# Fewer uncut score products, a first chunk of 64 rows and later low weights in a kernel of attention, feed-forward and mixture

## The chip, the core and the metric

The kernel runs on one core of a Trainium2 chip. The metric is the device time of one execution in microseconds (us). The engines are called TensorE (PE in the profile; its weight loads are PEld), VectorE (DVE), ScalarE (ACT), GpSimd (POOL) and SyncE (SP, which issues the transfers here).

## The reference

Three layers follow each other; each takes what the one before gives. Batch 4, sequence 448, model width 768.

```python
# 1. attention: 12 heads of 64, causal
scores = scale * np.matmul(q, k.transpose(0, 1, 3, 2))
scores = np.where(mask, -1000000000.0, scores)
scores = scores - np.max(scores, axis=-1, keepdims=True)
attn = np.exp(scores)
attn = attn / (np.sum(attn, axis=-1, keepdims=True) + 1e-09)
x = np.matmul(attn, v)
...
# 2. feed-forward with a gate from a convolution of 3 steps, width 1024
h = np.maximum(x @ w_in, 0.0)
for k in range(K):
    conv_out += conv_w[k][None, None, :] * hp[:, k:k + S, :]
gate = 1.0 / (1.0 + np.exp(-conv_out))
x = h * gate @ w_out
...
# 3. mixture: the best 2 of 4 experts for each position, each a causal attention head of 64
topk = np.argpartition(-(x @ w_gate), K, axis=-1)[..., :K]
for e in range(E):
    q, k, v = x @ wq[e], x @ wk[e], x @ wv[e]
    ...
    ye = a @ v @ wo[e]
    out += mask[..., None] * w[:, :, kk:kk + 1] * ye
```

All inputs are float32. The choice of experts hangs on small differences, so the products must hold nearly all of float32.

## The kernel before, in words

**Products in two halves.** A float32 matrix is cut into a high half, rounded to the fp32r type, and a low half, which is what is left (`high`, line 588, a copy; `low`, line 599, a subtraction). A product of two matrices is then three matmuls: high by high, low by high, high by low. A float32 matmul without the cut is also used, at four passes, where cutting is dearer.

**Pairs of heads.** Attention works on 24 pairs of heads, six a batch. For the pairs in `WHOLE_QK` (before: pairs 0 to 2 of the first batch) query and key are loaded as they are by `prepare_whole` (the keys in a sparse layout, by small transfers) and each score chunk is one float32 matmul a head (line 659). For the others `prepare` loads both, a high half of both is made (`ON["qk high"]`: VectorE, ScalarE or GpSimd) and two low halves (VectorE or GpSimd), and `scores` writes three matmuls a chunk and head (line 669), the two heads side by side, each with 64 rows of contraction.

**Chunks.** A pair's 448 query positions are cut in four chunks that begin at `Q0` = 0, 64, 192 and 320. Their widths `QN` are 64, 128, 128, 128, but before the change the first chunk is computed with 128 rows too, those of positions 0 to 127, and the keys up to 64. Each chunk takes a masked maximum on VectorE (line 644), an exponential on ScalarE (line 648) and a scaling by the row's sum (line 694 or 691). Then the weights are transposed on TensorE (`tr`, line 702) and multiplied by the values (`weigh`, line 761; `weigh_both`, line 747, with uncut float32 for the pairs in `WHOLE_AV`, the first eight). The transposes of the chunks are put side by side in one PSUM tile, so that those of a 128-row first chunk overlap the second's place and come before it.

**Feed-forward.** For each batch `ffn_in` makes eight groups of 18 products with 448 columns (line 896, into `pf`), each followed by: a relu on ScalarE (line 910, tile `hp`), three convolution steps (line 916 on ScalarE, 921 twice on VectorE, tile `half`), a tanh (line 936), a gate (line 929), and the gate's high and low halves (tile `pair`, lines 592 to 600). `ffn_out` makes six groups of 24 products from the eight gates and the output weights (tile `thou`), and stores its results to memory, from where the mixture loads them.

**Mixture.** `weights` (line 1021) loads the mixture's weights, makes their high halves (ScalarE or GpSimd) and their low halves (GpSimd alone), three loads for one tile `wbig` and then four for another. These start when the last attention pair's weights are scaled (`free`). Then follow, batch by batch, the queries and keys, values, four experts and the output.

**Order.** A class `Plan` collects every step with a cost for each engine that may do it. It runs a list scheduling with a rank for each step, several times, adds noise to the ranks of steps that begin in given stretches (`SHIFTS`: seed, from, to, amplitude), and writes the instructions in the order of the resulting plan. So the engine of a step, the buffers and the order of each engine's instructions come from that plan. A step begins on the chip when the data that it reads are there; a step behind it on its engine waits with it.

```python
        whole = p in WHOLE_QK
        ops = prepare_whole(p) if p in WHOLE_QK else prepare(p, ph, not whole)
        ...
        late = P.ops[-1]          # in the loop over batches: the last step of ffn_in
        ffn_out(b, gs)
        ...
        free = [NORM[B * H - 1]]  # behind the loop
```

Of the kernel before, what the change touches and what calls it, by code (L numbers as in the profile page):

```python
# [13 lines left out]
OP = mybir.AluOpType  # L14
# [24 lines left out]
WHOLE_QK = range(3)  # L39
# [11 lines left out]
SIDES = 3.6  # L51

# [15 lines left out]
def product(n):  # L68
    return 0.0034 + n * 0.000442
# [443 lines left out]
def attention_moe_moe(ctx: ExitStack, tc: tile.TileContext, qk, vv, w_in, cw, w_out, wqk, wvg, wo, out):  # L513
# [94 lines left out]
    def scores(qk, j, e, turns=False):  # L608
# [16 lines left out]
        def bank(o, c):  # L625
            return sbs[o][c][:, COL[c]:COL[c] + Q0[c] + QN[c]]

        def ec(o, c):
            n = Q0[c] + QN[c]
            if turns:  # L630
                return e[:, COL2[c]:COL2[c] + 2 * n].rearrange("p (j o d) -> p j o d", o=2, d=64)[:, :, o]
            return e[:, COL2[c] + o * n:COL2[c] + o * n + n]
# [5 lines left out]
        def weight(o, c):  # L638

            w, st, sb = Q0[c] + QN[c], sts[o], sbs[o]  # L640

            def mx(_):
                m = mask[:, 448 - w:448] if c and (o or turns) else mask[:, 320:320 + w]
                nc.vector.tensor_tensor_reduce(out=ec(o, c), in0=blocked(bank(o, c)), in1=blocked(m), scale=-0.125, scalar=3.0e38,  # L644
                                               op0=OP.add, op1=OP.min, accum_out=st[:, 0, c:c + 1])

            def ex(_):
                nc.scalar.activation(ec(o, c), ec(o, c), AF.Exp, bias=st[:, 0, c:c + 1], scale=-1.0,  # L648
                                     accum_out=st[:, 1, c:c + 1])

            P.op({"V": on_vector(w)}, mx, r=[(sb[c], c)], w=[(e, (o, c)), (st, ("m", c))])
            P.op({"A": on_scalar(w) + 0.23}, ex, r=[(st, ("m", c))], w=[(e, (o, c)), (st, ("s", c))])


        if whole:
            for o, (qs, kh, r) in enumerate(qk):
                for c in ORDER:
                    w = Q0[c] + QN[c]
                    P.op({"T": 4 * w / 2400}, lambda _, o=o, c=c, w=w, qs=qs, kh=kh: nc.tensor.matmul(
                        bank(o, c), qs()[:, Q0[c]:Q0[c] + 128], kh()[:, :w // 64], start=True, stop=True), r=r, w=[(sbs[o][c], c)])  # L660
                    weight(o, c)
        else:
            q, k, r = qk
            for two in (ORDER[:2], ORDER[2:]):
                def mm(_, two=two):
                    for c in two:
                        for i, (s, t) in enumerate(((0, 0), (1, 0), (0, 1))):
                            for o, own in enumerate(HALF):
                                nc.tensor.matmul(bank(o, c), q(s)[own, Q0[c]:Q0[c] + 128], k(t)[own, kc(o, c)], start=i == 0, stop=i == 2)  # L669

                P.op({"T": sum(SIDES * max(product(Q0[c] + QN[c]), 0.107) for c in two)}, mm, r=r,
                     w=[(sbs[o][c], c) for c in two for o in range(2)])
                for c in two:
                    for o in range(2):
                        weight(o, c)
# [4 lines left out]
    def norms(j, st, o, ec, e):  # L680
# [7 lines left out]
        for c in ORDER:  # L688
            def norm(en, c=c):
                if en == "A":  # L690
                    nc.scalar.activation(ec(o, c), ec(o, c), AF.Copy, scale=st[:, 3, c:c + 1])  # L691
                else:
                    gate = coef[:, b, c, x:x + 1] if moe else 1.0
                    engine(en).tensor_scalar(ec(o, c), ec(o, c), st[:, 3, c:c + 1], gate, op0=OP.mult, op1=OP.mult)  # L694
# [6 lines left out]
    def tr(dst, src, r, keys, m=128):  # L701
        P.op({"T": TURN}, lambda _: nc.tensor.transpose(dst(), src(), ident), r=r, w=keys, m=m)  # L702

    def transpose(e, p):
# [4 lines left out]

        for c in range(4):  # L710
            tr(lambda c=c: t0[:, Q0[c]:Q0[c] + 128], lambda n=COL2[c] + Q0[c] + QN[c]: e[:, n - 64:n + 64],
               [(e, (o, c)) for o in range(2)], [(t0, 0), (t0, 1)] if c == 0 else [(t0, c)])
# [17 lines left out]
    def weigh_both(e, v, v_r, dst):  # L730
# [3 lines left out]
        for i, use in enumerate(BLOCKS):  # L734
            t, a = P.buf("tb" if i in (1, 2) else "ta"), P.buf("ab")
            n = 0
            for j, col, q in use:
                for c in range((j + 1) // 2, 4):
                    m = COL2[c] + j * 128
                    tr(lambda t=t, x=col + Q0[c] - q: t[:, x:x + 128], lambda m=m: e[:, m:m + 128], [(e, (o, c)) for o in range(2)],  # L740
                       [(t, (j, c))] + ([(t, (j, 1))] if c == 0 else []))
# [280 lines left out]
    def weights(src, n, w, n0, keys):  # L1022
# [3 lines left out]
        P.op(copy_cost(n, "AG"), high(hi, lambda: raw[:, :n]), r=[(raw, 0)], w=[(w, (k, 0)) for k in keys])  # L1026
        P.op(two_cost(n, "G"), low(lo, lambda: raw[:, :n], hi), r=[(raw, 0)] + [(w, (k, 0)) for k in keys], w=[(w, (k, 1)) for k in keys])
# [211 lines left out]
```

## Time and profile before

| | |
|---|---|
| time, median of 3 runs (lowest to highest) | 605.22 us (605.09 to 607.0) |
| the profiled execution's own time | 602.88 us |
| its span, first to last instruction | 601.1 us |
| granted clock of TensorE | 1.00 |
| busy: PE, PEld, DVE, ACT, POOL | 577.9, 505.1, 479.0, 404.4, 190.8 us |
| share of the span | 96, 84, 80, 67, 32% |
| costliest group | 984 products of `ffn_in` and the mixture's projections, 219.8 us |
| moved by DMA | 87.78 MB, 146 GB/s |

Busy time is the union of an engine's instructions. Matmuls overlap in the records: each lasts longer than the distance to the next, so a group's sum of durations is more than its place on the engine. An idle time is put down to the step that ended last before it (the releaser). The tile names in the rows are those of buffers: `pair` holds a high and a low half, `half` raw data or convolution results, `full` raw loads, `e` the attention weights, `a` their transposes.

### The profile page before, as it was taken

Reading aid. Unit: us, or ns where it says so; the run is one execution under the profiler, and the core shown is the slowest. Engines: PE = TensorE matmul, PEld = TensorE weight load, DVE = VectorE, ACT = ScalarE, POOL = GpSimd, SP = SyncE. Lnnn points to the kernel's source line nnn. Section 1 sums busy time; section 2 is a strip of 40 time slices with the busy share of each in tenths; the row PEclk is TensorE's granted clock in tenths of the full one; section 3 lists DMA queues with packets and bytes.
Section 4 is the critical chain, followed back from the end, with each engine's and each line's share of the span. In section 5 each row is a group of like instructions: output and inputs, shape, how many; then the busy total and the mean of one; then the engine's idle time right before and its main releaser. Section 6 shows DMA issues by size and latency. Waiting matters only on the chain.

```text
span 601.1 us, 10782 instructions
## 1 busy us (share of the span) xinstructions
PE 577.9 (96%) x3577; PEld 505.1 (84%) x3580; DVE 479.0 (80%) x1353; ACT 404.4 (67%) x1035; POOL 190.8 (32%) x207
## 2 busy tenths in 40 slices
PE   8899989899999999999999999979999999999987
PEld 4577778788888988898999998868999989999877
DVE  6999999999998879987979985981156569649993
ACT  4688469888889658968868984451133268456973
POOL 4443532555663014543201631750001023002510
PEclk9999999999999999999999999999999999999999
DMA  8455534478880065672038629509733400200113
GB/s 246 146 137 150 151 103 148 131 268 286 275 270 17 1 194 190 213 256 42 2 112 270 216 89 390 136 26 352 252 92 119 152 33 2 93 1 2 63 71 145
DMA packets 50457, 87.78 MB, mean 146 GB/s; under 512 B 21856, under 2 KB 31456, under 8 KB 50400
## 3 DMA queue, kind: packets, MB, share of 16 engines
q1 hardware_dynamic: 50400, 87.09, 44.6%
q8 instruction: 28, 0.46, 0.3%
q14 instruction: 29, 0.24, 0.1%
HBM read 64.26 MB, written 22.81 MB: 145 GB/s over the span
## 4 chain that ended last, share of the span: by engine, by line
PE 56%; DVE 7%; ACT 2%; DMA 1%; issue 1%; SPq 0%; POOL 0%; ACTq 0%
PE pf L896 40%; PE po L761 5%; PE t L702 5%; PE sx L669 4%; DVE pair L600 1%; DVE half L921 1%; DMA thou<-w_scratch 1%; DVE a L600 1%; DVE e L644 1%; PE sy L669 1%; DVE half L773 1%; ACT pair L592 1%; ACT hp L910 0%; PE t L896 0%; DVE half L929 0%
## 5 line engine op out<-in xcount | busy, mean ns | idle before, releaser
L896 PE MATMUL pf<-pair,wbig 128*128 128x448 f32 x984 | 219.8, 371 | 6.2 <-ACT hp L910 3.8
L896 PEld LDWEIGHTS pf<-pair,wbig 128*128 128x128 f32 x984 | 180.2, 188 | 24.4 <-ACT hp L910 5.9
L648 ACT ACTIVATE e<-e,stat 128x448 f32<-128x448 f32 (+3 forms) x256 | 127.2, 499 | 29.0 <-DVE stat L644 28.2
L896 PE MATMUL pf<-pair,thou 128*128 128x448 f32 x576 | 131.1, 374 | 5.8 <-DVE pair L600 4.4
L896 PEld LDWEIGHTS pf<-pair,thou 128*128 128x128 f32 x576 | 105.1, 188 | 15.7 <-DVE pair L600 5.4
L600 DVE TENSOR_TENSOR a<-t,a 64x448 fp32r<-64x448 f32 (+1 forms) x96 | 75.5, 787 | 10.9 <-ACT a L592 8.8
L702 PE MATMUL t<-ident,e 128*128 128x128 f32 x512 | 81.9, 275 | 1.7 <-DVE e L694 0.7
L592 ACT ACTIVATE a<-t 64x448 fp32r<-64x448 f32 (+1 forms) x96 | 64.4, 674 | 16.5 <-PE t L702 11.2
L600 DVE TENSOR_TENSOR pair<-pf,pair 128x448 fp32r<-128x448 f32 (+3 forms) x56 | 30.1, 552 | 52.3 <-ACT pair L592 51.8
L702 PEld LDWEIGHTS t<-ident,e 128*128 128x128 f32 x512 | 61.4, 141 | 9.6 <-DVE half L594 1.2
L592 ACT ACTIVATE pair<-pf 128x448 fp32r<-128x448 f32 (+3 forms) x56 | 26.3, 486 | 59.2 <-PE pf L896 57.7
L761 PE MATMUL po<-a,thou 128*128 128x384 f32 (+5 forms) x336 | 64.3, 309 | 1.1 <-DVE half L773 1.1
L694 POOL TENSOR_SCALAR e<-e,stat,coef 128x192 f32<-128x192 f32 (+3 forms) x37 | 21.9, 605 | 131.3 <-DVE stat L687 57.7
L644 DVE CUSTOM_DVE_ANT_0 e<-sx,mask 128x64 f32<-128x64 f32 (+3 forms) x128 | 51.4, 416 | 6.1 <-PE sy L669 5.4
L921 DVE SCALAR_TENSOR_TENSOR half<-hp,cws,half 128x448 f32<-128x448 f32 x64 | 49.0, 779 | 8.2 <-ACT half L916 7.9
L644 DVE CUSTOM_DVE_ANT_0 e<-sy,mask 128x320 f32<-128x320 f32 (+3 forms) x128 | 50.7, 416 | 5.0 <-PE sy L669 3.4
L761 PEld LDWEIGHTS po<-a,thou 128*128 128x128 f32 (+1 forms) x336 | 47.6, 173 | 5.4 <-DVE half L773 2.6
L669 PE MATMUL sx<-pair,pair 64*128 64x448 f32 (+3 forms) x264 | 50.4, 306 | 0.1
L669 PE MATMUL sy<-pair,pair 64*128 64x448 f32 (+3 forms) x264 | 50.3, 306 | 0.0
L691 ACT ACTIVATE e<-e,stat 128x320 f32<-128x320 f32 (+3 forms) x104 | 46.8, 507 | 5.0 <-DVE stat L687 3.5
L648 ACT ACTIVATION_READ_ACCUMULATOR e<-e,stat 128x1 f32 x256 | 48.3, 189 | 0.0
L669 PEld LDWEIGHTS sx<-pair,pair 64*128 64x128 f32 x264 | 41.5, 185 | 4.6 <-issue 2.2
(109 smaller groups left out, 895.1 us busy)
## 6 DMA issues: line engine op xcount, KB each, us to landing
thou<-w_scratch SPq DMA_DIRECT2D x36, 512.0 KB, 5.4
x_scratch<-pair SPq DMA_DIRECT2D x24, 448.0 KB, 5.2
pair<-x_scratch SPq DMA_DIRECT2D x24, 448.0 KB, 6.0
full<-in_w_in SPq DMA_DIRECT2D x12, 512.0 KB, 4.2
full<-in_w_out SPq DMA_DIRECT2D x12, 512.0 KB, 4.8
w_scratch<-thou SPq DMA_DIRECT2D x12, 512.0 KB, 4.7
out<-half SPq DMA_DIRECT2D x24, 224.0 KB, 1.9
half<-in_vv SPq DMA_DIRECT2D x16, 256.0 KB, 4.6
```

The source lines that it names most:

```text
L592: nc.scalar.activation(dst(), src(), AF.Copy)
L600: return lambda e: engine(e).tensor_sub(dst(), src(), f32(h()))
L644: nc.vector.tensor_tensor_reduce(out=ec(o, c), in0=blocked(bank(o, c)), in1=blocked(m), scale=-0.125, scalar=3.0e38, op0=OP.add, op1=OP.mi ...
L648: nc.scalar.activation(ec(o, c), ec(o, c), AF.Exp, bias=st[:, 0, c:c + 1], scale=-1.0, accum_out=st[:, 1, c:c + 1])
L669: nc.tensor.matmul(bank(o, c), q(s)[own, Q0[c]:Q0[c] + 128], k(t)[own, kc(o, c)], start=i == 0, stop=i == 2)
L691: nc.scalar.activation(ec(o, c), ec(o, c), AF.Copy, scale=st[:, 3, c:c + 1])
L694: engine(en).tensor_scalar(ec(o, c), ec(o, c), st[:, 3, c:c + 1], gate, op0=OP.mult, op1=OP.mult)
L702: P.op({"T": TURN}, lambda _: nc.tensor.transpose(dst(), src(), ident), r=r, w=keys, m=m)
L761: lambda _: nc.tensor.matmul(ps[:n, q:S], v(k, m), rhs(), start=start, stop=stop),
L773: P.op({"V": on_vector(S)}, lambda _: nc.vector.tensor_add(xf[HALF[o], :S], ps[:64, :S], xc[HALF[0], :S]), r=[(ps, 0), (xc, 0)], w=[(xf, o)])
L896: nc.tensor.matmul(out_ap(), a(), b(), start=first, stop=end), r=r, w=[(ps, 0)])
L921: return lambda _: nc.vector.scalar_tensor_tensor(cv[:, :S], hp[:, i:S + i], cws[:, fc, i:i + 1], cv[:, :S], op0=OP.mult, op1=OP.add)
```

## The change

1. `WHOLE_QK` holds pair 0 alone; pairs 1 and 2 go through `prepare` and have cut score products.
2. The first chunk has 64 rows in all its steps: scores, masked maximum, exponential, scaling and transposes. Its transpose takes 64 rows of contraction and writes 64 columns, and no longer overlaps the second chunk's.
3. The mixture's high weights are made by ScalarE alone, and each low half waits for `late`, the low half of the last gate of the last `ffn_in`.
4. The planner's cost of a score group is another, `SHIFTS` has 37 other entries, and so the whole order is new.

```diff
-WHOLE_QK = range(3)
+WHOLE_QK = range(1)
...
-SIDES = 3.6
...
-    (50226, 530, 540, 1), (2079, 416, 436, 2), (83136, 282, 292, 1), (43264, 499, 539, 1), (58582, 209, 229, 1),
+    (42011, 517, 527, 2), (39824, 301, 321, 2), (93157, 66, 86, 5), (8490, 203, 243, 0.5), (81995, 460, 470, 2),
...
         def bank(o, c):
-            return sbs[o][c][:, COL[c]:COL[c] + Q0[c] + QN[c]]
+            return sbs[o][c][:QN[c], COL[c]:COL[c] + Q0[c] + QN[c]]
...
-            return e[:, COL2[c] + o * n:COL2[c] + o * n + n]
+            return e[:QN[c], COL2[c] + o * n:COL2[c] + o * n + n]
...
-                        bank(o, c), qs()[:, Q0[c]:Q0[c] + 128], kh()[:, :w // 64], start=True, stop=True), r=r, w=[(sbs[o][c], c)])
+                        bank(o, c), qs()[:, Q0[c]:Q0[c] + QN[c]], kh()[:, :w // 64], start=True, stop=True), r=r, w=[(sbs[o][c], c)])
...
-                                nc.tensor.matmul(bank(o, c), q(s)[own, Q0[c]:Q0[c] + 128], k(t)[own, kc(o, c)], start=i == 0, stop=i == 2)
-
-                P.op({"T": sum(SIDES * max(product(Q0[c] + QN[c]), 0.107) for c in two)}, mm, r=r,
+                                nc.tensor.matmul(bank(o, c), q(s)[own, Q0[c]:Q0[c] + QN[c]], k(t)[own, kc(o, c)], start=i == 0, stop=i == 2)
+
+                P.op({"T": 0.09 + sum(3 * max(product(Q0[c] + QN[c]), QN[c] / 1200) for c in two)}, mm, r=r,
...
-    def tr(dst, src, r, keys, m=128):
-        P.op({"T": TURN}, lambda _: nc.tensor.transpose(dst(), src(), ident), r=r, w=keys, m=m)
+    def tr(dst, src, r, keys, n=128):
+
+        P.op({"T": TURN}, lambda _: nc.tensor.transpose(dst()[:, :n], src()[:n], ident[:n, :n]), r=r, w=keys)
...
-               [(e, (o, c)) for o in range(2)], [(t0, 0), (t0, 1)] if c == 0 else [(t0, c)])
+               [(e, (o, c)) for o in range(2)], [(t0, c)], QN[c])
...
-                       [(t, (j, c))] + ([(t, (j, 1))] if c == 0 else []))
+                       [(t, (j, c))], QN[c])
...
-        P.op(copy_cost(n, "AG"), high(hi, lambda: raw[:, :n]), r=[(raw, 0)], w=[(w, (k, 0)) for k in keys])
-        P.op(two_cost(n, "G"), low(lo, lambda: raw[:, :n], hi), r=[(raw, 0)] + [(w, (k, 0)) for k in keys], w=[(w, (k, 1)) for k in keys])
+        P.op(copy_cost(n, "A"), high(hi, lambda: raw[:, :n]), r=[(raw, 0)], w=[(w, (k, 0)) for k in keys])
+
+        P.op(two_cost(n, "G"), low(lo, lambda: raw[:, :n], hi), r=[(raw, 0)] + [(w, (k, 0)) for k in keys], w=[(w, (k, 1)) for k in keys],
+             after=[late])
```

The lines that are left out slice the masks, the sums and the scaling to `QN[c]` rows in the same way. In the changed kernel line numbers from 649 on are one lower (895 for 896), and from `weights` on one higher.

How the order of the instructions moves is shown at three places. The first is GpSimd around the last convolution: `pair` with `half` are low halves of gates, `wbig` with `full` the mixture's weights (L596 is a high half, L600 a low one). Before:

```order
L596 TENSOR_SCALAR pair_107<-half_135 128x448
L600 TENSOR_TENSOR pair_107<-half_135,pair_107 128x448
L600 TENSOR_TENSOR pair_112<-half_137,pair_112 128x448
L596 TENSOR_SCALAR wbig_104<-full_133 128x1024
L596 TENSOR_SCALAR wbig_104<-full_132 128x1024
L600 TENSOR_TENSOR wbig_104<-full_134,wbig_104 128x1024
L600 TENSOR_TENSOR wbig_104<-full_133,wbig_104 128x1024
L600 TENSOR_TENSOR wbig_104<-full_132,wbig_104 128x1024
L600 TENSOR_TENSOR wbig_105<-full_134,wbig_105 128x780
L600 TENSOR_TENSOR wbig_105<-full_133,wbig_105 128x780
L600 TENSOR_TENSOR wbig_105<-full_132,wbig_105 128x768
```

With the change:

```order
L600 TENSOR_TENSOR pair_124<-half_136,pair_124 128x448
L596 TENSOR_SCALAR pair_110<-half_140 128x448
L600 TENSOR_TENSOR pair_110<-half_140,pair_110 128x448
L600 TENSOR_TENSOR pair_111<-half_136,pair_111 128x448
L600 TENSOR_TENSOR wbig_104<-full_133,wbig_104 128x1024
L600 TENSOR_TENSOR wbig_104<-full_132,wbig_104 128x1024
L600 TENSOR_TENSOR wbig_104<-full_134,wbig_104 128x1024
L600 TENSOR_TENSOR wbig_105<-full_133,wbig_105 128x780
L600 TENSOR_TENSOR wbig_105<-full_132,wbig_105 128x780
L600 TENSOR_TENSOR wbig_105<-full_134,wbig_105 128x768
```

Two high halves of the weights have left GpSimd; its low halves of gates are three here instead of two, with a high half between them, and the low halves of the weights follow the last of them.

The second is TensorE at one pair of heads of the last batch: L702 are transposes of the weights `e`, L761 (L760 with the change) products with the values. Before:

```order
L702 MATMUL t_143<-ident,e_156 128x128 x4
L761 MATMUL po_162<-a_158,thou_130 128x448
L761 MATMUL po_162<-a_159,thou_130 128x256
L761 MATMUL po_162<-a_159,thou_130 128x384
L761 MATMUL po_162<-a_159,thou_130 128x128
L761 MATMUL po_162<-a_159,thou_130 64x128
L761 MATMUL po_162<-a_159,thou_130 64x256
L702 MATMUL t_144<-ident,e_156 128x128 x2
L761 MATMUL po_162<-a_159,thou_130 128x384
L702 MATMUL t_144<-ident,e_156 128x128 x4
```

With the change:

```order
L760 MATMUL po_162<-a_158,thou_130 128x448
L760 MATMUL po_162<-a_159,thou_130 128x256
L760 MATMUL po_162<-a_159,thou_130 128x384
L702 MATMUL t_143<-ident,e_156 128x64
L760 MATMUL po_162<-a_159,thou_130 128x128
L702 MATMUL t_143<-ident,e_156 128x128 x2
L702 MATMUL t_144<-ident,e_156 128x128
L702 MATMUL t_143<-ident,e_156 128x128
L760 MATMUL po_162<-a_159,thou_130 64x128
L760 MATMUL po_162<-a_159,thou_130 64x256
L760 MATMUL po_162<-a_159,thou_130 128x384
L702 MATMUL t_144<-ident,e_156 128x128 x5
```

One transpose of the pair has become a 64-row one (128x64), and here it stands by itself between products of full height; the others are as before, in another order.

The third is VectorE at the start of the kernel: L644 are masked maxima (each in two rows, the second of 128x1 or 64x1), L861 to L865 (L860, L862) cut a weight of the feed-forward part, and L600 makes the low halves of a pair's query and key. Before:

```order
L861 TENSOR_SCALAR half_136<-full_132 128x512
L863 SCALAR_TENSOR_TENSOR half_136<-full_132,half_136 128x512
L865 SCALAR_TENSOR_TENSOR half_136<-full_132,half_136 128x512
L594 CAST wbig_104<-half_136 128x512
L644 ISA e_155,stat_82<-sy_161,mask 128x5x64
L644 ISA stat_82 128x1
L644 ISA e_155,stat_82<-sy_161,mask 128x3x64
L644 ISA stat_82 128x1
L644 ISA e_155,stat_82<-sx_160,mask 128x7x64
L644 ISA stat_82 128x1
L644 ISA e_155,stat_82<-sx_160,mask 128x64
L644 ISA stat_82 128x1
```

With the change:

```order
L600 TENSOR_TENSOR pair_107<-full_132,pair_106 128x448 x2
L644 ISA e_155,stat_82<-sx_160,mask 128x7x64
L644 ISA stat_82 128x1
L644 ISA e_155,stat_82<-sx_160,mask 64x64
L644 ISA stat_82 64x1
L860 TENSOR_SCALAR half_136<-full_133 128x512
L644 ISA e_155,stat_82<-sy_161,mask 128x5x64
L644 ISA stat_82 128x1
L644 ISA e_155,stat_82<-sy_161,mask 128x3x64
L644 ISA stat_82 128x1
L862 SCALAR_TENSOR_TENSOR half_136<-full_133,half_136 128x512
```

The two low halves of pair 1 now come first, before any maximum, and the first chunk's maximum covers 64 rows.

## Rows read from the trace of the kernel before

**Rows 1.** Busy time by stretches. Columns: us; busy us and (instructions) of five engines; PEclk, DMA share, GB/s.

```profile
30.00:45.00 15.00, 14.54 (x96) 11.16 (x96) 14.96 (x65) 13.20 (x45) 7.41 (x10) 1.00 0.50 138
...
240.00:270.00 30.00, 30.00 (x208) 26.74 (x208) 26.70 (x71) 24.41 (x61) 14.81 (x18) 1.00 0.72 229
```

**Rows 2.** Timeline of TensorE, 366 to 425 us. Start us, us, instruction, [idle before <-releaser].

```profile
369.09 18.47 PE L896 MATMUL pf<-pair,wbig 128*128 128x448 f32 x90 [0.44 <-ACT hp L910]
388.69 3.91 PE L896 MATMUL pf<-pair,wbig 128*128 128x448 f32 x18 [1.13 <-ACT hp L910]
...
401.09 4.92 PE L896 MATMUL pf<-pair,thou 128*128 128x448 f32 x23 [3.27 <-DVE pair L600]
407.11 18.10 PE L896 MATMUL pf<-pair,thou 128*128 128x448 f32 x88 [1.10 <-DVE pair L600]
```

**Rows 3.** Timeline of GpSimd in the same stretch.

```profile
378.96 8.15 POOL L600 TENSOR_TENSOR wbig<-full,wbig 128x1024 fp32r<-128x1024 f32 x3 [0.66 <-ACT wbig L592]
```

**Rows 4.** Timeline of VectorE in the same stretch.

```profile
379.42 2.70 DVE L600 TENSOR_TENSOR pair<-half,pair 128x448 fp32r<-128x448 f32 x1
```

**Rows 5.** Tile half on VectorE, 375 to 406 us. Times are ns: min/median/max.

```profile
L921 DVE SCALAR_TENSOR_TENSOR half<-hp,cws,half x12: 671/684/2821, 374.6 to 401.0; 128x448 f32<-128x448 f32 x12
```

**Rows 6.** Costliest groups, from the page. Columns: busy us, mean ns | idle before, releaser.

```profile
L896 PE MATMUL pf<-pair,wbig 128*128 128x448 f32 x984 | 219.8, 371 | 6.2 <-ACT hp L910 3.8
```

**Rows 7.** Timeline of TensorE around a score group, 281 to 287 us.

```profile
280.84 3.20 PE L896 MATMUL pf<-pair,wbig 128*128 128x448 f32 x15
283.97 0.41 PE L669 MATMUL sx<-pair 64*128 64x320 f32 x1
...
284.92 2.30 PE L896 MATMUL pf<-pair,wbig 128*128 128x448 f32 x10
```

**Rows 8.** Timeline of TensorE at three transpose groups.

```profile
58.02 1.47 PE L702 MATMUL t<-ident,e 128*128 128x128 f32 x12
...
303.81 0.71 PE L702 MATMUL t<-ident,e 128*128 128x128 f32 x5
304.44 0.46 PE L669 MATMUL sx<-pair 64*128 64x448 f32 x1
...
324.09 0.66 PE L702 MATMUL t<-ident,e 128*128 128x128 f32 x4
```

**Rows 9.** Timeline of TensorE, the end of one score group.

```profile
305.18 0.27 PE L669 MATMUL sx<-pair,pair 64*128 64x64 f32 x1
...
305.29 0.27 PE L669 MATMUL sx<-pair,pair 64*128 64x64 f32 x1
305.50 0.70 PE L896 MATMUL pf<-pair,thou 128*128 128x448 f32 x2
```

**Rows 10.** Timeline of TensorE, a change of output columns alone.

```profile
352.28 0.60 PE L761 MATMUL po<-a,thou 128*64 128x128 f32 x3
...
356.93 0.42 PE L761 MATMUL po<-a,thou 128*128 128x384 f32 x1
```

**Rows 11.** Timeline of TensorE: uncut scores of one pair, then cut scores of another.

```profile
8.98 1.03 PE L659 MATMUL sy<-block,half 128*128 128x320 f32 x4
...
10.76 4.91 PE L987 MATMUL pf<-mask 128*128 128x512 bf16 x21
...
34.12 0.47 PE L669 MATMUL sx<-pair 64*128 64x448 f32 x1
...
35.18 2.33 PE L747 MATMUL po<-half,block 128*128 128x384 f32 x10
37.44 0.41 PE L669 MATMUL sx<-pair 64*128 64x320 f32 x1
...
38.39 0.59 PE L747 MATMUL po<-half,block 128*128 128x192 f32 x2
```

**Rows 12.** Groups by line with shapes kept apart. Columns as in rows 6.

```profile
L600 POOL TENSOR_TENSOR pair<-full,pair 128x448 fp32r<-128x448 f32 x25 | 30.5, 1229 | 8.0 <-ACT pair L592 4.4 <-DVE pair L594 2.7 <-DMA x_scratch<-pair 0.6
...
L600 DVE TENSOR_TENSOR pair<-full,pair 128x448 fp32r<-128x448 f32 x17 | 12.4, 736 | 0.1
```

More of the change, by code (lines that the diff above doesn't have):

```diff
@@ L630, in ec @@
             if turns:
-                return e[:, COL2[c]:COL2[c] + 2 * n].rearrange("p (j o d) -> p j o d", o=2, d=64)[:, :, o]
-            return e[:, COL2[c] + o * n:COL2[c] + o * n + n]
+                return e[:QN[c], COL2[c]:COL2[c] + 2 * n].rearrange("p (j o d) -> p j o d", o=2, d=64)[:, :, o]
+            return e[:QN[c], COL2[c] + o * n:COL2[c] + o * n + n]
         def kc(o, c):
@@ L638, in weight @@
         def weight(o, c):
-            w, st, sb = Q0[c] + QN[c], sts[o], sbs[o]
+            w, st, sb, rows = Q0[c] + QN[c], sts[o], sbs[o], slice(0, QN[c])
             def mx(_):
-                m = mask[:, 448 - w:448] if c and (o or turns) else mask[:, 320:320 + w]
+                m = mask[rows, 448 - w:448] if c and (o or turns) else mask[rows, 320:320 + w]
                 nc.vector.tensor_tensor_reduce(out=ec(o, c), in0=blocked(bank(o, c)), in1=blocked(m), scale=-0.125, scalar=3.0e38,
-                                               op0=OP.add, op1=OP.min, accum_out=st[:, 0, c:c + 1])
+                                               op0=OP.add, op1=OP.min, accum_out=st[rows, 0, c:c + 1])
             def ex(_):
-                nc.scalar.activation(ec(o, c), ec(o, c), AF.Exp, bias=st[:, 0, c:c + 1], scale=-1.0,
-                                     accum_out=st[:, 1, c:c + 1])
+                nc.scalar.activation(ec(o, c), ec(o, c), AF.Exp, bias=st[rows, 0, c:c + 1], scale=-1.0,
+                                     accum_out=st[rows, 1, c:c + 1])
             P.op({"V": on_vector(w)}, mx, r=[(sb[c], c)], w=[(e, (o, c)), (st, ("m", c))])
@@ L690, in norm @@
                 if en == "A":
-                    nc.scalar.activation(ec(o, c), ec(o, c), AF.Copy, scale=st[:, 3, c:c + 1])
+                    nc.scalar.activation(ec(o, c), ec(o, c), AF.Copy, scale=st[:QN[c], 3, c:c + 1])
                 else:
-                    gate = coef[:, b, c, x:x + 1] if moe else 1.0
-                    engine(en).tensor_scalar(ec(o, c), ec(o, c), st[:, 3, c:c + 1], gate, op0=OP.mult, op1=OP.mult)
+                    gate = coef[:QN[c], b, c, x:x + 1] if moe else 1.0
+                    engine(en).tensor_scalar(ec(o, c), ec(o, c), st[:QN[c], 3, c:c + 1], gate, op0=OP.mult, op1=OP.mult)
             cost = scale_cost(Q0[c] + QN[c])
```

12 rows, old and new, of the table SHIFTS are left out of this document.

## The prediction, made before the changed kernel ran

> **What bounds the kernel now.** I began with the busy time by stretches. In the first stage VectorE is full (14.96 of 15 us between 30 and 45 us) and TensorE has gaps; later TensorE is full (30.00 of 30 us) while VectorE has more than 3 us to spare [rows 1]. So an edit in the first stage counts by what it does to VectorE, and every nanosecond between matmuls counts after some 120 us.
>
> Next I read TensorE's own timeline for the places where it is not full late on. Around the last feed-forward input stage it stands for 1.13, 3.27 and 1.10 us, the last two behind VectorE's low halves of the gates [rows 2]. In the same stretch GpSimd makes the low halves of the mixture's weights, three in 8.15 us [rows 3]. Beside them a low half of a gate takes 2.70 us [rows 4] and one convolution step 2.82 us, where the median of the twelve steps of that stretch is 684 ns [rows 5]. A VectorE instruction there lasts as long as the GpSimd instruction beside it; the two hold each other up, and TensorE waits behind.
>
> Last, the spacing of matmuls, read from start to start. A 448-column product comes every 0.203 us ((18.47 - 0.37) / 89, with a record of 371 ns) [rows 2, 6]. Where TensorE goes from full-height matmuls to those on 64 rows and back, it loses time at both ends: 15 products take 3.13 us to the first score product, 0.08 more than 15 x 0.203, and the ten after the scores take 2.30 us, 0.10 more than 9 x 0.203 + 0.37 [rows 7]. For transposes the pitch is 0.109 us ((1.47 - 0.71) / 7), five of them need 0.63 to the first score product, 0.09 more than five pitches, and four behind a score group take 0.66, 0.06 more than an undisturbed four [rows 8]. Leaving costs as well: score products of 64 columns start 0.11 us apart, the first full-height product behind them 0.21 after the last, 0.10 more [rows 9]. A change of columns alone costs nothing: the three matmuls from 64 output columns back to 128 run 0.60 us from the first start to the last end, and 128 + 256 columns at the full rate and a last record of 0.42 give just that [rows 10].
>
> **The change, part by part.** The sum is made against the profiled execution, 602.88 us (span 601.1 and 1.8 around it); it lies 2.3 below the median of the runs shown, 605.22, so the same difference is taken off the median.
>
> *The mixture's low weights wait.* They now stand behind the last gate of the last convolution, and the high halves are ScalarE's alone. What goes is the hold-up beside them [rows 4, 5], and with it up to 1.13 + 3.27 + 1.10 = 5.5 us [rows 2]. With VectorE free, TensorE has 36 products (7.3 us) that need none of the last two gates, which is longer than the chain of the last convolution. The 1.13 may stay, since it ended with ScalarE, which now makes three high halves in a row there. Bounds -5.5 and -3.3; I take -5.2, near the upper end because two of the three waits are put down to VectorE itself. What is late next: the first three low halves now run some 8 us behind the last gate, and the second matrix's loads stand on the queue behind four stores of results. The cover is the output stage, 144 products or 29 us, and after it four more query and key groups (14 us) that don't use the second matrix. Without that cover 8.15 us would be open; I cost it at nothing.
>
> *First chunk of 64 rows, in the transposes.* Each of the 32 pairs of heads (24 of the attention, 8 of the mixture's experts) has one transpose that now contracts over 64 rows, so it is a 64-row matmul among full-height ones. In the new order TensorE changes its row height 184 times, 116 before; 8 of the 68 more are the two extra score pairs. A lone one costs 0.09 going in, 0.10 coming out and 0.06 for the one behind it, 0.25 in all [rows 8, 9]. Of the 32, six lie in the first stage, where TensorE waits anyway, two stand directly behind score products and one in the tail's idle time; 23 x 0.25 = +5.7. Nothing in the trace shows a 64-row transpose: the lower bound is entry and exit alone at the smallest rows, 23 x 0.17 = +3.9 (nothing at all is a rival below), the upper 0.08 + 0.10 + 0.10 with products behind it and some more lost on the second load, 0.35 x 23 = +8.
>
> *First chunk of 64 rows, in the scores.* Its three products a head move 64 columns but start 0.11 us apart, because 128 columns of weights are loaded for each [rows 9]. With 64 columns loaded the pitch can fall towards half. Per pair I take -0.08 (bounds 0 and -0.11), 26 pairs behind the first stage: -2.1 (0 to -2.9). VectorE and ScalarE gain nothing: their time goes with columns, which stay at 64.
>
> *Two pairs of the first stage with cut score products.* Uncut, a pair takes 2 x 1.78 = 3.56 us of TensorE, cut 1.06 + 0.95 = 2.01 [rows 11]; two pairs give back 3.1 us. It falls where VectorE is the bound. Added are two high halves (ScalarE) and four low ones: by the new order VectorE makes the first pair's two (2 x 736 ns) before its first maximum, GpSimd the other's (2 x 1229 ns) [rows 12]. The small, scattered key loads go. VectorE's list up to the last convolution of the first batch is as long as before. Bounds -3.1 (all of TensorE's gain) and +3.7 (three more GpSimd lows in the stage, each holding VectorE as in [rows 4]); I take -0.5, near the middle.
>
> *New order.* VectorE has 1330 rows instead of 1347 and GpSimd 225 instead of 205. Where TensorE is full [rows 1] the order is worth little; nothing is taken for it.
>
> Sum: -5.2 + 5.7 - 2.1 - 0.5 = **-2.1**, that is 600.8 for such an execution and **603.1** for the median.
>
> **A rule weighed.** The Trainium skill, "TensorEngine Tiling (Array Packing)", section Tiling Modes, says that changing the tiling mode, not just the tile, drains TensorE. It speaks against this change; the rows agree for row heights [rows 7, 8] and not for columns [rows 10]. By the rule the step inside the scores from 128 to 64 output columns would drain too, which is the first rival.
>
> **The rivals.** What a measurement of this kernel can tell from no change is 0.3%, or 1.8 us.
>
> 1. *The narrow chunk drains as well (slower).* The scores' fourth chunk goes from 64 x 128 to 64 x 64 tiles. If that costs what a change of height costs (0.10 coming in, and 0.10 on the load behind), each pair loses 0.12 instead of gaining 0.08: 26 x 0.2 = 5.2 more, 608.3. It decides from about 0.2 us a pair on. Against it: rows 10, though those are full-height. Chance 0.13.
> 2. *The lone transposes are nearly free (much faster).* All losses at a change of height were read where two heads' products run side by side. If a single 64-row transpose costs only 0.05, 4.6 go: 598.5. For it: TensorE loads ahead between transposes and products elsewhere. Against: the entry loss comes before any second head. Chance 0.15.
> 3. *The wait at the last convolution is replaced (no change).* ScalarE's three high halves in a row, or a late gate, keep about 2.2 of the 5.5: 605.0. Against: 3.27 stood directly behind VectorE. Chance 0.20.
> 4. *GpSimd's larger share slows VectorE in the first stage.* 3.7 us more where VectorE is full [rows 1, 4], and 0.5 less gained: 607.3. Against: VectorE's list is no longer there than before. Chance 0.12.
>
> **How the numbers follow.** The forecast has 0.40; its own range, by the bounds of the first three terms, is 600.5 to 605.5, so about two thirds of it lie beyond the 1.8 us. Faster: 0.27 + 0.15 + 0.03 (rival 3) = 0.45. Within 0.3%: 0.13 + 0.16 + 0.03 = 0.32. Slower: 0.13 + 0.09 + 0.01 = 0.23. The range 598.0 to 608.5 takes in the forecast, rivals 3 and 4 and about half of the first two, a little over 8 in 10.
>
> **What would show it.** In the changed profile the waits of rows 2 should shrink to under 1 us together and no convolution step there should exceed 1 us; GpSimd's weight lows should stand at about 395 to 405 us and later. Around each 64-row transpose the neighbours' starts should lie 0.20 apart, not 0.11; the scores' 64-column products should be under 0.09 apart, with no 0.2 in front of them. In the first 120 us VectorE should be as full as now. The prediction is wrong if TensorE still stands for 3 us behind a gate, if it waits for low weights at the mixture's start, if lone transposes show no loss, or if the first stage grows by more than 2 us.

## The result and the profile after

| | before | changed |
|---|---|---|
| time, median | 605.15 us | 596.18 us (595.56 to 596.49) |
| ratio | | 0.9852, 95% interval 0.982 to 0.9884 |
| the profiled execution's own time | 602.88 us | 596.44 us |
| its span | 601.1 us | 594.7 us |
| busy: PE, DVE, POOL | 577.9, 479.0, 190.8 us | 576.4, 467.4, 205.6 us |

Faster by 9.0 us, where 2.1 were forecast; the time lies below the range (598.0 to 608.5). (The median of before has a fourth run in it now, 605.15 for the 605.22 of the prediction.) Between the two profiled executions the difference is 6.4 us, between the medians 9.0; that gap of 2.6 is one of the findings below.

TensorE's timeline of the changed kernel around the last convolution answers to [rows 2]:

```profile
368.20 22.11 PE L895 MATMUL pf<-pair,wbig 128*128 128x448 f32 x108 [0.43 <-ACT hp L909]
390.98 29.47 PE L895 MATMUL pf<-pair,thou 128*128 128x448 f32 x144 [0.67 <-ACT hp L909]
```

The waits of 1.13, 3.27 and 1.10 us have become one of 0.67 (that of 0.44 is still there, as 0.43), and the 144 products of the output stage run through. GpSimd's timeline there answers to [rows 3]:

```profile
365.89 1.15 POOL L600 TENSOR_TENSOR pair<-half,pair 128x448 fp32r<-128x448 f32 x1 [6.20 <-DMA thou<-w_scratch]
378.06 7.98 POOL L600 TENSOR_TENSOR wbig<-full,wbig 128x1024 fp32r<-128x1024 f32 x3 [11.02 <-ACT wbig L592]
418.50 1.86 POOL L600 TENSOR_TENSOR wbig<-full,wbig 128x780 fp32r<-128x780 f32 x1 [32.46 <-ACT wbig L592]
```

The first three low halves were **not** made to wait: they run from 378 us, as before, 19 us before the last gate's low half, which VectorE starts at 397.2 us. `after=[late]`, point 3 of the change, holds only in the planner. On the chip GpSimd waits for its data, here for ScalarE's high halves, and then goes. What moved is the second matrix: from 394 us to 418 us. In the kernel before, its low halves on GpSimd stood beside the steps of the last two gates on VectorE:

```profile
394.27 6.29 POOL L600 TENSOR_TENSOR wbig<-full,wbig 128x780 fp32r<-128x780 f32 x3 [7.16 <-ACT wbig L592]
...
394.39 4.51 DVE L921 SCALAR_TENSOR_TENSOR half<-hp,cws,half 128x448 f32<-128x448 f32 x2
398.82 2.21 DVE L600 TENSOR_TENSOR pair<-half,pair 128x448 fp32r<-128x448 f32 x1
```

Two convolution steps took 4.51 us and a low half 2.21, where the medians there are 0.68 a step [rows 5] and 0.62 a low half. ScalarE's timeline of the changed kernel shows why the group is later, its high halves now wait for a load that arrives then:

```profile
417.57 0.86 ACT L592 ACTIVATE wbig<-full 128x780 fp32r<-128x780 f32 x1 [1.40 <-DMA full<-in_wvg]
```

The first group still holds VectorE up; tile `half` on VectorE, 375 to 406 us, has the same longest step as [rows 5]:

```profile
L920 DVE SCALAR_TENSOR_TENSOR half<-hp,cws,half x11: 671/681/2827, 374.4 to 394.7; 128x448 f32<-128x448 f32 x11
```

So here a hold-up of 2.8 us, while several gates were still to come, went with no wait of TensorE over 0.67 us; beside the last two gates, before, such hold-ups went with waits of 3.27 and 1.10 us [rows 2].

TensorE at transposes and at the end of a score group (to be held against [rows 8] and [rows 9]):

```profile
53.18 1.72 PE L702 MATMUL t<-ident,e 128*128 128x128 f32 x12
...
488.97 0.27 PE L702 MATMUL t<-ident,e 64*128 64x64 f32 x1
489.17 1.07 PE L895 MATMUL pf<-pair,wbig 128*128 128x448 f32 x4
...
270.54 0.22 PE L668 MATMUL sx<-pair,pair 64*64 64x64 f32 x1
...
270.60 0.22 PE L668 MATMUL sx<-pair,pair 64*64 64x64 f32 x1
270.76 1.07 PE L895 MATMUL pf<-pair,wbig 128*128 128x448 f32 x4
```

Twelve transposes, one of them on 64 rows, take 1.72 us where twelve of full height took 1.47: 0.25 more, as the working had it for one. A lone one between products keeps the next away for 0.20. The 64-column products start 0.06 us apart (0.11 before), and the first product behind them comes after 0.16 (0.21).

The first stage, busy time by stretches:

```profile
15.00:30.00 15.00, 14.72 (x100) 10.26 (x98) 14.38 (x53) 13.01 (x42) 11.46 (x12) 1.00 0.54 149
30.00:45.00 15.00, 15.00 (x108) 11.90 (x106) 14.93 (x51) 14.13 (x40) 8.35 (x9) 1.00 0.48 145
```

VectorE is as full as in [rows 1], but TensorE is now full beside it: 15.00 of 15 us where it had 14.54, and between 15 and 30 us 14.72 where it had 12.65. In that earlier stretch 2.9 us are fillers (products of zeros, `pf<-mask`; 1.0 us before), so there TensorE is full partly by them; both kernels run 25 of them in the first stage.

What the first stage gained is seen at the first product of the first output stage. TensorE's timelines there, of before, changed, e13 and e14 (the last two are told below):

```profile
101.72 2.60 PE L896 MATMUL pf<-pair,thou 128*128 128x448 f32 x12
...
96.33 1.07 PE L895 MATMUL pf<-pair,thou 128*128 128x448 f32 x4 [0.35 <-ACT hp L909]
...
99.56 1.09 PE L899 MATMUL pf<-pair,thou 128*128 128x448 f32 x4 [0.35 <-ACT hp L913]
...
101.00 3.20 PE L896 MATMUL pf<-pair,thou 128*128 128x448 f32 x15
```

The changed kernel is there 5.4 us earlier, with the same 144 input products behind it. That is the greater part of the 6.4 us between the profiled executions.

### The profile page after: what moved, and what is told of

It is laid out like the page before. It is cut to its first block, busy times and chain, and to the rows that moved or that the text cites. A ratio compares the mean times of both kernels' runs of the same rounds, so it can differ in the third digit from the quotient of the medians.

```text
span 594.7 us, 10838 instructions
## 1 busy us (share of the span) xinstructions
PE 576.4 (97%) x3596; PEld 497.8 (84%) x3596; DVE 467.4 (79%) x1334; ACT 406.3 (68%) x1037; POOL 205.6 (35%) x229
## 5 line engine op out<-in xcount | busy, mean ns | idle before, releaser
L895 PE MATMUL pf<-pair,wbig 128*128 128x448 f32 x984 | 215.6, 369 | 4.2 <-ACT hp L909 2.0
L648 ACT ACTIVATE e<-e,stat 128x448 f32<-128x448 f32 (+3 forms) x256 | 127.1, 499 | 24.3 <-DVE stat L644 23.8
L702 PE MATMUL t<-ident,e 128*128 128x128 f32 (+1 forms) x512 | 85.4, 276 | 3.5 <-DVE a L600 1.7
L600 DVE TENSOR_TENSOR a<-t,a 64x448 fp32r<-64x448 f32 (+1 forms) x96 | 75.4, 786 | 9.3 <-ACT a L592 7.3
L702 PEld LDWEIGHTS t<-ident,e 128*128 128x128 f32 (+1 forms) x512 | 62.4, 140 | 18.8 <-issue 7.5
L600 DVE TENSOR_TENSOR pair<-pf,pair 128x448 fp32r<-128x448 f32 (+3 forms) x56 | 30.3, 552 | 57.3 <-ACT pair L592 56.9
L760 PE MATMUL po<-a,thou 128*128 128x384 f32 (+5 forms) x336 | 64.3, 310 | 1.4 <-DVE half L772 1.0
L600 POOL TENSOR_TENSOR pair<-half,pair 128x448 fp32r<-128x448 f32 x29 | 35.1, 1210 | 86.0 <-ACT half L592 33.2
L644 DVE CUSTOM_DVE_ANT_0 e<-sx,mask 128x320 f32<-128x320 f32 (+3 forms) x128 | 51.1, 413 | 13.2 <-PE sy L668 11.0
L644 DVE CUSTOM_DVE_ANT_0 e<-sy,mask 128x320 f32<-128x320 f32 (+3 forms) x128 | 51.0, 413 | 1.0 <-PE t L702 0.5
L760 PEld LDWEIGHTS po<-a,thou 128*128 128x128 f32 (+1 forms) x336 | 47.2, 174 | 4.8 <-DVE half L772 1.7
L690 ACT ACTIVATE e<-e,stat 128x448 f32<-128x448 f32 (+3 forms) x105 | 47.3, 506 | 5.5 <-DVE stat L686 3.6
L668 PE MATMUL sx<-pair,pair 64*128 64x320 f32 (+3 forms) x280 | 50.3, 294 | 0.0
L668 PE MATMUL sy<-pair,pair 64*128 64x320 f32 (+3 forms) x280 | 50.2, 294 | 0.0
L648 ACT ACTIVATION_READ_ACCUMULATOR e<-e,stat 128x1 f32 (+1 forms) x256 | 48.4, 189 | 0.0
L600 POOL TENSOR_TENSOR pair<-full,pair 128x448 fp32r<-128x448 f32 x28 | 35.2, 1267 | 34.5 <-ACT pair L592 24.2
```

Of the source, the lines that this page charges most:

```text
L600: return lambda e: engine(e).tensor_sub(dst(), src(), f32(h()))
L648: nc.scalar.activation(ec(o, c), ec(o, c), AF.Exp, bias=st[rows, 0, c:c + 1], scale=-1.0, accum_out=st[rows, 1, c:c + 1])
L668: nc.tensor.matmul(bank(o, c), q(s)[own, Q0[c]:Q0[c] + QN[c]], k(t)[own, kc(o, c)], start=i == 0, stop=i == 2)
L702: P.op({"T": TURN}, lambda _: nc.tensor.transpose(dst()[:, :n], src()[:n], ident[:n, :n]), r=r, w=keys)
L760: lambda _: nc.tensor.matmul(ps[:n, q:S], v(k, m), rhs(), start=start, stop=stop),
L895: nc.tensor.matmul(out_ap(), a(), b(), start=first, stop=end), r=r, w=[(ps, 0)])
```

## The experiments

The changed kernel was not run again beside these runs. The kernel before was, and its medians lie between 604.76 and 605.34 us, so a difference to the changed kernel's 596.18 carries some tenths of a us from that.

**Two parts of the change, taken back in the changed kernel's own order.** In e1 the transposes have full height again:

```diff
-        nc.tensor.transpose(dst()[:, :n], src()[:n], ident[:n, :n])
+        def full(t):   # n == 64: columns 0..63 and the unused 448..511 of the PSUM tile
+            return t if n == 128 else t.rearrange("p (b c) -> p b c", c=64)[:, 0:8:7]
+        nc.tensor.transpose(full(dst()), src(), ident)
```

> The changed kernel with the same order, but the first chunk's transposes have 128 rows again: the 64 spare rows of each weights tile are zeroed once, and the 64 columns that come of them go to the unused end of the PSUM tile. Theory (a lone 64-row transpose costs 0.25 us, as its neighbours' starts in the changed trace say, 0.20 + 0.20 + 0.165 for 3 x 0.109): 23 of 32 count, so 5 to 6 us less than the changed kernel, about 590.5. Rival (the engine catches up between transposes and products, as rival 2 had it): within 1 us of the changed kernel, 595 to 597.

Measured: 591.71 us, ratio to before 0.9788 (0.9756 to 0.982): 4.5 less than the changed kernel, so the 64-row transposes cost +4.5. The first theory holds, a little smaller: 4.5 is what 18 of the 32 come to at 0.25 us each, not 23. In e1 the first product of the first output stage starts at 94.65 us (96.33 in the changed kernel), so 1.7 us of it arise in the first stage. Twelve transposes are back at 1.47 us in e1's timeline:

```profile
51.99 1.47 PE L708 MATMUL t<-ident,e 128*128 128x128 f32 x12
```

This version beats both kernels by a clear margin.

```diff
-  q(s)[own, Q0[c]:Q0[c] + QN[c]]
+  q(s)[own, Q0[c]:Q0[c] + 128]     # e2, into 128 rows of the bank
```

> The changed kernel with the same order, but the cut score products of the first chunk load 128 columns of queries again and write 128 rows (64 of them unused). Theory (the pitch of a 64-column product goes back from 0.05 to 0.10 us and the way out from 0.15 to 0.20, 0.106 a pair): 26 pairs behind the first stage, 2.5 to 3 us more than the changed kernel, about 599. Rival (the gain per pair is taken back by the step to a narrower tile elsewhere): within 0.7 us of it.

Measured: 598.51 us, 2.3 more. The narrow scores are worth -2.3; the rival falls.

**The mixture's weights, in both directions.** e3 puts the old two lines back into the changed kernel, e4 the new two into the kernel before (the diff is that of e4; e3 is the same the other way round):

```diff
-        P.op(copy_cost(n, "AG"), high(...), ...)
-        P.op(two_cost(n, "G"), low(...), ...)
+        P.op(copy_cost(n, "A"), high(...), ...)
+        P.op(two_cost(n, "G"), low(...), ..., after=[late])
```

> The changed kernel with the mixture's weights as before (high halves on ScalarE or GpSimd, low halves without the wait for the last gate); the order is the changed kernel's up to the last convolution. Theory (the low halves of the weights beside the last gates cost TensorE its waits): the waits around the last feed-forward input stage come back, 3 to 6 us more, 599 to 602. Rival (the new order alone took the waits away): no wait over 1.5 us there, and a time within 1.5 us of the changed kernel.

> The kernel before with the new handling of the mixture's weights alone; its order is that of before up to the last convolution. Theory: the 3.27 and 1.10 us waits go, 4 to 5.5 us less than before, about 600. Rival (the waits go by the order, not by the weights): at least 3 us of waits stay there, and the time is within 1.5 us of before.

Measured: e3 603.62 us, 7.4 more than the changed kernel (ratio to before 0.9971); e4 598.91 us, 6.0 less than before (0.9901, 0.9869 to 0.9932). Both are theory, and both larger than it said (3 to 6, and 4 to 5.5). TensorE in e3, then in e4:

```profile
388.11 3.91 PE L895 MATMUL pf<-pair,wbig 128*128 128x448 f32 x18 [1.58 <-ACT hp L909]
...
396.31 5.74 PE L895 MATMUL pf<-pair,thou 128*128 128x448 f32 x26 [1.45 <-DVE pair L600]
```

```profile
369.69 22.10 PE L896 MATMUL pf<-pair,wbig 128*128 128x448 f32 x108 [0.43 <-ACT hp L910]
392.24 29.45 PE L896 MATMUL pf<-pair,thou 128*128 128x448 f32 x144 [0.44 <-ACT hp L910]
```

The waits come and go with these two lines. In e4, too, the first group runs beside the gates (380.50 us, 7.89 us) and the second at 418.94. Not all of the two differences are these waits: by the last output product e3 is 5.0 us behind the changed kernel, and the rest comes later, where its order is new too; and e4 has a mean granted clock of 0.997, where the runs of before beside it have 0.994.

e5 was to move the second group alone:

```diff
+    def weights(src, n, w, n0, keys, wait=()):   # wait=[late] for wvg and wo only
+        P.op(copy_cost(n, "A" if wait else "AG"), ...)
+        P.op(two_cost(n, "G"), low(...), ..., after=wait)
```

> The kernel before, and of the mixture's weights only those of the second matrix are handled in the new way (high halves on ScalarE alone, planned behind the last gate); the first matrix's are made as before, its two high halves on GpSimd too. Theory A (the second group of low halves, 394 to 401 us in the trace of before, held up the last gate): the waits of 3.27 and 1.10 go, that of 1.13 stays, 4 to 5 us less than before. Theory B (the first group, 379 to 387 us, which the prediction named, delays the gates): at least 3 us of waits stay, within 2 us of before.

Measured: 604.66 us, ratio 0.999 (0.9963 to 1.0018), no change. The edit did not move what it meant to: the planner put the low halves behind the last gate, but their loads and high halves kept their places, and on the chip GpSimd went on as soon as those were there. Its timeline, and then TensorE's:

```profile
396.93 6.28 POOL L600 TENSOR_TENSOR wbig<-full,wbig 128x780 fp32r<-128x780 f32 x3 [7.17 <-ACT wbig L592]
```

```profile
395.14 5.34 PE L896 MATMUL pf<-pair,thou 128*128 128x448 f32 x25
403.74 6.48 PE L896 MATMUL pf<-pair,thou 128*128 128x448 f32 x23 [3.27 <-DVE pair L600]
```

With the group in its old place the old wait is there. So e5 doesn't tell theory A from B by itself; with e4, where the first group ran beside the gates and no wait over 0.44 us was left, it speaks for A. No run moved the second group alone; e4 also takes two high halves off GpSimd.

**The order and the uncut pairs.** e6, e7 and e8 change one table or one range (`WHOLE_QK`, `SHIFTS = ()`) and are planned anew, as are e10 to e12 (e11 and e12 change both).

> The changed kernel with three uncut pairs as before; the order is planned anew. Theory A (cut products for two pairs are worth what TensorE saves and more in the first stage): 3 to 5 us more than the changed kernel, and already there at the first product of the first output stage. Theory B (VectorE bounds that stage, as the prediction had it): within 1.5 us of the changed kernel, 595 to 597.5.

> The kernel before with one uncut pair instead of three, nothing else; the order is planned anew. Theory A: 3 to 5 us less than before, 600 to 602. Theory B: within 1.5 us of before.

> The changed kernel with an empty table of noise, so with the planner's own order. Theory A (where TensorE is full the order is worth little, as the prediction had it): within 1.5 us of the changed kernel. Theory B (the chosen noise is worth several microseconds): 2 to 5 us more, and then the rest of the gain that no part explains can come from the new table.

> The kernel before with an empty table of noise, to be held against the changed kernel without noise (601.6). Theory A (the table of before is worth as much as that of the changed kernel, 5 us): 608 to 612, so the parts of the change alone carry 7 to 10 us. Theory B (the table of before was worth little, and the new one is where the unexplained 4 us come from): 604 to 606.

> The kernel before without noise and with one uncut pair. Theory A (cut products for the two pairs gain what TensorE saves, whatever the order): 3 to 5 us less than the kernel before without noise. Theory B (VectorE bounds the first stage): within 1.5 us of it.

> The changed kernel without noise and with three uncut pairs. Theory A: 3 to 5 us more than the changed kernel without noise (601.6). Theory B: within 1.5 us of it.

| | noise kept | no noise |
|---|---|---|
| before, three uncut | 605.15 | 610.70 (e10) |
| before, one uncut | 615.32 (e7) | 615.64 (e11) |
| changed, three uncut | 610.58 (e6) | 611.31 (e12) |
| changed, one uncut | 596.18 | 601.60 (e8) |

A table that fits its kernel is worth about 5.5 us to both: theory B of e8, a little larger, and theory A of e10. Without noise the change is worth 9.1 us (610.70 to 601.60), as with it, so a luckier table is not where the gain comes from. One uncut pair instead of three costs 5 to 10 us in the old design and saves 10 to 14 in the new one: neither theory, in e6, e7, e11 and e12. A plan made anew can bring stands of its own (in e6 and e12 one of 3.3 us at about 328 us, behind VectorE, which the changed kernel hasn't), so these four mix the pairs with the lot that was drawn.

Hence two runs in unchanged orders. e13 pads TensorE at pairs 1 and 2 of the changed kernel; e14 thins it there in the kernel before: of the 1024 score columns of a head it computes 448, the first ones of each chunk:

```diff
+                    if j in (2, 4):               # e13, ahead of each score group
+                        for sb in (sbs[0][two[0]], sbs[1][two[0]]):
+                            for _ in range(2):
+                                nc.tensor.matmul(sb[:, :], zeros[:, :128], zeros[:, :512], start=True, stop=True)
...
-                        bank(o, c), ..., kh()[:, :w // 64]
+                        bank(o, c)[:, :w if j == 0 else w // 128 * 64 or 64], ..., kh()[:, :w // 64 if j == 0 else w // 128 or 1]   # e14
```

> The changed kernel in its own order, with four idle matmuls of 512 columns (0.22 us each) ahead of each of the four score groups of pairs 1 and 2, written to the score tiles themselves, so that TensorE is as long at these pairs as with uncut products (1.73 us more a pair). Theory A (TensorE's saving at the two pairs reaches the end): 2.5 to 3.5 us more than the changed kernel, 598.7 to 599.7. Theory B (TensorE has room there, and the gain of the first stage came from the order or from VectorE): within 0.8 us of it.

> The kernel before in its own order; at the uncut pairs 1 and 2 only the first 448 of 1024 score columns of a head are computed (the rest is left out), so TensorE spends about 1.6 us on a pair instead of 3.56. Theory A: 3 to 4 us less than before, 601 to 602. Theory B: within 1 us of before.

Measured: e13 600.56 us, 4.4 more than the changed kernel: theory A, there, and more than its 2.5 to 3.5. Its first output stage begins 3.2 us later (99.56 for 96.33), nearly all of the 16 idle matmuls (3.5 us). e14 605.44 us, ratio 1.0002 (0.998 to 1.0023): theory B, in the order before. TensorE's microseconds at these pairs reach the end in one order, and net of everything nothing comes of them in the other.

Two things can take them in the order before, and e14 doesn't part them. One is TensorE's clock, which e14 doesn't hold fixed. Its twelve executions have a mean granted clock of 0.989 to 0.994, 0.991 on average, where the runs of before beside it have 0.995. Over 600 us that is some 2 us, by my estimate, of the 3 to 4 that were to be saved. Its profiled execution shows one such place (columns as in [rows 1]):

```profile
20.00:23.00 3.00, 1.94 (x12) 1.81 (x13) 3.00 (x15) 2.27 (x8) 0.00 (x0) 0.92 0.52 127
23.00:26.00 3.00, 3.00 (x9) 1.93 (x8) 2.07 (x9) 3.00 (x13) 1.99 (x3) 0.51 0.92 263
```

Six products with the values take 2.79 us there, 1.78 in the profiled execution of before, whose clock is 1.00. For all that, e14's first output stage begins 0.7 us earlier than that of before (101.00 for 101.72). Over the first 100 us TensorE is busy for 90.87 us in e14 and for 91.46 before, so only 0.6 us of the saving became longer stands; in this execution the clock took more.

The other is VectorE. Its timeline in the kernel before, with GpSimd's of the same stretch behind it, shows a knot:

```profile
15.32 2.72 DVE L694 TENSOR_SCALAR e<-e,stat 128x64 f32<-128x64 f32 x2
17.97 2.16 DVE L600 TENSOR_TENSOR pair<-full,pair 128x448 fp32r<-128x448 f32 x2
20.05 0.48 DVE L644 CUSTOM_DVE_ANT_0 e<-sy,mask 128x320 f32<-128x320 f32 x1
```

```profile
14.95 2.82 POOL L600 TENSOR_TENSOR wbig<-half,wbig 128x512 fp32r<-128x512 f32 x2
17.72 1.38 POOL L600 TENSOR_TENSOR thou<-half,thou 128x512 fp32r<-128x512 f32 x1
```

For 4.7 us VectorE does four instructions, beside GpSimd's, while the score banks wait for their maxima at 20.05; TensorE stands there for 2.00 us, before and in e14, whether its scores took long or not, and in e14 waits of 0.52 and 0.84 us behind the scaling (line 694) come ahead of it. In the changed order VectorE has made eight maxima between 15.7 and 20.4 us. That this knot, and not another place of the first stage, is what the new order undid is read from the traces and was not tried by itself.

**The spread of before.** e9 puts idle matmuls into two stands of TensorE in the kernel before:

```diff
+   keep("uncut", 1, pft[1], 8)   # 8 matmuls of zeros ahead of the second head's scores of pair 1
+   keep("out", 26, sxt[0], 10)   # 10 ahead of the 26th product of the last output stage
```

> The kernel before in its own order, with idle matmuls (of zeros, into PSUM tiles that nobody reads) in its two longest stands of TensorE: 8 of them at about 19 us, 10 at about 398 us; the stands themselves stay as long. Of 39 listed executions of before 38 show a mean granted clock under 1 (0.989 to 0.997), the profiled one does not; the changed kernel shows 0.999 or 1.00 in all. Theory A (the stands cost a second time, by a lower clock behind them): clock 0.998 or more in nearly all runs, 2 to 3 us less than before, 601.5 to 602.5. Theory B (the spread of before has nothing to do with its stands): clock and time as before, 604 to 605.5.

Measured: 603.51 us, ratio 0.997 (0.9954 to 0.9986), 1.8 less than before, with a clock of 0.997 to 1.00 in every run where the runs of before beside it had 0.991 to 1.00. Theory A, with a smaller size than expected (2 to 3 us; the interval is 0.8 to 2.8).

## Why the prediction was wrong

By its own steps, with what the runs gave in place of each:

| step | taken | measured |
|---|---|---|
| low weights wait | -5.2 | -6.0 (e4; taken out again, e3: 7.4) |
| transposes of 64 rows | +5.7 | +4.5 (e1) |
| narrow scores | -2.1 | -2.3 (e2) |
| two cut pairs, new order | -0.5 | -5.2, what is left of -9.0 (-3.8 with e3's 7.4) |

- **The term that failed is the last one**: "I take -0.5, near the middle", and "nothing is taken for it" of the order. The first output stage begins 5.4 us earlier (96.33 for 101.72), though the 64-row transposes cost 1.7 us there. Both sentences rested on one stage being full on VectorE and the others on TensorE [rows 1]. A full VectorE said nothing of *which* of its instructions the score banks waited for. In the order before, the thinner scores are worth nothing net (e14), near what I said, but there the clock takes a share that I had not counted; in the new order TensorE is full beside VectorE, and its saving goes through (e13). I priced the edit in the order that it replaced. The bound of -3.1, all of TensorE's gain, was even passed, since stands went as well: TensorE is busy for 94.41 of the first 100 us, where it was for 91.46. How the gain divides between the cut score products and the order is not shown beyond e13, and whether the order freed it by undoing the knot stays open.
- **"The same difference is taken off the median" failed too.** The profiled execution of before had a clock of 1.00 and 602.88 us, and the median was 2.3 above it. Of 80 listed executions of before in the experiments 75 show a mean granted clock of 0.989 to 0.997. The changed kernel lacks these stands, has a clock of 0.999 or 1.00 in all four executions, and a median that lies 0.3 below its profiled execution. At least in part the 2.3 were a cost of the stands that I was removing: 1.8 us come back when idle matmuls fill two of them (e9). The 2.6 between the medians' 9.0 and the profiles' 6.4 are these 2.3 and 0.3, and they sit in the -6.0 and the -5.2 of the table.
- **The convolution**: the size held (-5.2 against -6.0, with some clock in it), the mechanism only in part. I named the first group of low halves and its 8.15 us [rows 3]; it still stands where it stood. The second group, beside the last two gates, goes with the waits (e4, e5). I also took a planner's `after` for a wait of the chip. The 1.13 behind ScalarE went as well, to 0.67.
- **The transposes**: 0.25 each, as worked out [rows 8, 9]; their sum is that of 18 rather than 23. Those of the first stage, which I left out because TensorE "waits anyway" there, do count (1.7 us, e1): the same error as in the last term.
- **The range**: by the bounds of the first three terms it is 600.2 to 609.4, not "600.5 to 605.5"; the 596.18 lies below both.
- The rule that I weighed held where the rows did. By the Trainium skill, "TensorEngine Tiling (Array Packing)", section Tiling Modes, a changed tiling mode drains TensorE. In this trace a step to fewer columns did not (0.06 between starts), a change of rows did (0.20 between starts on either side of a 64-row transpose, where 0.11 is usual).
- Of the signs named, three came true: 0.20 around the 64-row transposes, under 0.09 between narrow products, VectorE as full as before in the first stage. One nearly did: the waits of [rows 2] are 1.10 us together (0.43 and 0.67), where under 1 was said. Two did not: a convolution step still lasts 2.8 us, and the first low halves stand at 378 us, not at 395 or later.
- The rivals: the narrow chunk doesn't drain (1), lone transposes aren't free (2), 1.1 us of waits are left and not 2.2 (3), GpSimd's larger share (205.6 us for 190.8) didn't slow the first stage, which ended 5.4 us earlier (4). None had the new order as the gain.

## What to carry to other kernels

A removed cost is worth what its engine's queue lets through in the *new* order: where the order moves too, read which instruction the waiting engine needs next, not how full the engine ahead of it is. Compare the profiled execution's clock with the clocks of the timed runs before a difference between profiles is put on a median. The same holds for an experiment that thins an engine: look at its clock before its null is read as "the engine had room". And in a kernel like this keep a matmul's row height: e1 has all of the change but the low transposes and is the fastest of all.

## What the hardware showed unexpectedly

A stand of TensorE can cost a second time. In e5 the stand of 3.27 us was followed by 23 products in 6.48 us, where the profiled execution of before has 4.92 behind the same stand [rows 2]. The stretches of e5 (columns as in [rows 1]):

```profile
20.00:23.00 3.00, 1.73 (x5) 1.45 (x6) 2.51 (x10) 2.02 (x7) 0.05 (x1) 0.78 0.45 121
23.00:26.00 3.00, 3.00 (x13) 2.09 (x13) 1.93 (x11) 2.07 (x9) 0.94 (x1) 0.65 0.45 147
400.00:405.00 5.00, 1.74 (x7) 1.22 (x6) 4.90 (x5) 1.27 (x2) 3.21 (x2) 0.90 0.00 0
405.00:410.00 5.00, 5.00 (x21) 4.42 (x19) 2.50 (x5) 0.14 (x1) 0.00 (x0) 0.76 0.00 0
```

The granted clock falls to the lower of its two levels (1.2 GHz) for part of the stretch behind each stand, 1.6 us lost at the second. It comes in one execution and not in the next: the kernel before stands for 2.00 and 3.27 us there and has 1.00 in these stretches of its profiled execution, and its listed executions range from 0.989 to 1.00 in the mean. In e3 shorter stands (1.58, 1.45, 1.09 us) left the clock at 1.00 in the profiled execution.
